# Attention heads in alternating half-array products: the two heads' scores by 64 rows, their products with v by 64 columns in float32

## The chip, the cores and the metric

The kernel runs on one core of a Trainium2 chip. The metric is the device time of one launch in microseconds (us). The time before is 1052.7 us, the median of three runs (1052.44 to 1053.11). The profile is of one more execution, which took 1059.5 us.

## What is computed

Block-causal attention (4 batches, 8 heads, 576 tokens, head dimension 64), and two feed-forward layers on its result (2304 tokens, 512 wide, 2048 in the middle):

```python
scores = 1.0 / np.sqrt(D) * np.matmul(q, k.transpose(0, 1, 3, 2))
mask = (pos[:, None] // 64) >= (pos[None, :] // 64)
scores = np.where(mask, scores, -1000000000.0)
attn = np.exp(scores - np.max(scores, axis=-1, keepdims=True))
attn = attn / (np.sum(attn, axis=-1, keepdims=True) + 1e-09)
x = np.matmul(attn, v)        # then (B, H, S, D) -> (B * S, H * D)
h = x @ moe_w_in;   x = (h * np.cos(h)) @ moe_w_out
h = x @ moe2_w_in;  r = np.maximum(h, 0.0);  out = (r * r) @ moe2_w_out
```

## The kernel before

All matmuls but the transposes and some products with v use float32r operands, each number split into a high part and a low part; a product is then three matmuls, high x high, high x low and low x high, summed in PSUM (`mm3`, L760).

**Order.** The kernel is first recorded as a list of operations with their reads and writes (`Recorder`, L136). A planner (`schedule`, L213) then places them on the engines by assumed costs and priorities, chooses the engine where several can do an operation, and assigns the 8 PSUM banks ("s" for scores, "t" for transposes, "a" for products with v, "h" and "y" for the feed-forward layers; at most five "s" and one "a" at a time). The program on each engine is in the planner's order, and every engine waits in that order. SyncE (SP) alone issues the DMAs.

**Attention.** A unit is a pair of heads of one batch; its 128 rows of transposed q or k hold the first head in rows 0 to 63 (`TOP`) and the second in rows 64 to 127 (`BOT`). Batch 0 is cut into region 1 (tokens 0 to 255, units 0 to 3) and region 2 (tokens 256 to 575, units 4 to 7), so that the feed-forward layer can begin early; batches 1 to 3 are units 8 to 19, each with both regions. `prep` (L856) transposes k and q and splits them: high and low keys `kh`, `kl`, queries `sa`, `sb`. Scores of a block of 128 queries go over 128, 256, 384 or 512 keys; the last 64 tokens of both heads are done together by `tail` tiles. DVE takes the row maximum (`soft_min`), ACT the exponential, POOL mostly the division; the result e is transposed on TensorE (PE) into r1 and r2 (`unit_transpose`, L992), and `unit_av` (L1024) multiplies it with v into xt, which is stored to x_d and split for the first layer.

Two switches decide how a unit is computed. `APART` (L31): in region 1 of batch 0 (and in units below 4) the scores of a head are three 64-row products, one head after the other. In all others, `both` (L864) copies each head's high keys into both halves of a tile (`ka`, `kb`), and its low keys into a tile whose other half is zero (`kz0a` to `kz1b`), by six DMAs per unit, and a head's scores are two products over all 128 rows:

```python
matmul(t[:, o:o + n], u.S[h][:, c], u.K[h][:, 0:n], True, False, holds=(e, st))
matmul(t[:, o:o + n], u.S[h][:, c], u.S[3][h][:, 0:n], False, True)
```

`PLAIN` (L30): units 0 to 7 multiply r with v as plain float32 into 64 columns of PSUM rows, one head after the other, and the profile shows two records for each such product. Units 8 to 19 split r into high and low (`r1l`, `r2l`, on DVE) and v into `vs` (`prep_v`, L841), compute 128 columns (v high and v low) for each, and add the two halves by a copy to `xb` on ACT and an addition on DVE.

k, q and v of a unit have one buffer each (`NATB = 1`, L33). The weights of the first layer arrive as `raw`, in two buffers (L666), and pass through ACT, POOL and DVE.

Of the kernel before, what the change touches and what calls it, by code (L numbers as in the profile page):

```python
# [29 lines left out]
PLAIN = 8  # L30
APART = 4  # L31
E1 = 7
# [313 lines left out]
def kernel(  # L346
# [264 lines left out]
    for i in range(2):  # L611
# [5 lines left out]

        pads = [T(sb, [128, 576], F32R, f"kz{i}{j}") for j in "ab"]
        memset(f(pads[0][64:128]), 0.0)
        memset(f(pads[1][0:64]), 0.0)  # L620
        QS.append((sa, sb_, tails, pads))
# [193 lines left out]
    def load_pair(b, p, part):  # L815
# [3 lines left out]
        u.apart = part == 1 or len(units) < APART  # L819
# [36 lines left out]
    def prep(u):  # L856

        kn, qn, vn = u.nat
        sa, sb_, tails, pads = u.S = QS[u.i % 2]
        ka, kb, kl, kh = u.K = tuple(T(sb, [128, 576], F32R, n, 2) for n in ("ka", "kb", "kl", "kh"))  # L860
# [5 lines left out]
        def both(which):  # L866
            if u.apart:
                return
            for i, h in enumerate((TOP, BOT)):
                if which == "h":  # L870
                    for g in (TOP, BOT):
                        dma(f(u.K[i][g]), f(kh[h]), 147456, 600.0)
                else:
                    dma(f(pads[i][h]), f(kl[h]), 147456, 600.0)

        def queries(t, c):
            if u.apart:

                act(sa[:, c], t, ACTF.Copy, scale=scale)
                stt(sb_[:, c], t, scale, f(sa[:, c]), ALU.mult, ALU.subtract)  # L880
                return
# [13 lines left out]
        else:  # L895
# [7 lines left out]
            both("h")  # L903
            lo_part(kl[:, 512:576], t[:, 0:64], kh[:, 512:576])
            both("l")
# [19 lines left out]
    @of("scores")  # L925
    def unit_scores(u, kind):

        e = T(sb, [128, 576], F32, "e", E1)
        st = T(sb, [128, 8], F32, "st", 6)
        if kind == "P":  # L930
            for j in range(2):
                t = bank("s")
                kc = slice(j * 288, j * 288 + 288)
                (th, tl), kl, kh = u.S[2], u.K[2][:, kc], u.K[3][:, kc]
                for i, (l, r) in enumerate(((th, kh), (th, kl), (tl, kh))):
                    matmul(t[:, 0:288], l, r, i == 0, i == 2, holds=(e, st))
                soft_min(e[:, kc], t[:, 0:288], mask[:, 0:288], st[:, 2 + j:3 + j])
            tt(st[:, 0:1], st[:, 2:3], st[:, 3:4], ALU.min)
            parts = [(0, 576)]
        else:  # L940
            h, ts_ = kind
            half = (TOP, BOT)[h]
            t = bank("s")
            parts, o = [], 0
            for j in ts_:
                n = 128 * (j + 1)
                c = slice(j * 128, j * 128 + 128)
                if u.apart:

                    (qh, ql), (kl, kh) = [x[half, c] for x in u.S[:2]], [x[half, 0:n] for x in u.K[2:]]  # L950
                    for i, (l, r) in enumerate(((qh, kh), (qh, kl), (ql, kh))):
                        matmul(t[:, o:o + n], l, r, i == 0, i == 2, holds=(e, st))
# [425 lines left out]
```

## Time and profile before

| | |
|---|---|
| median of the runs | 1052.7 us |
| profiled execution | 1059.5 us, span 1057.7 us |
| PE busy | 1020.6 us (96%) |
| DVE busy | 698.7 us (66%) |
| ACT busy | 676.7 us (64%) |
| POOL busy | 376.7 us (36%) |

Attention lies in the first 400 us of the span, among the first layer's first half; the rest is feed-forward layers only. A matmul's duration in the profile is from start to modelled end; successive matmuls overlap, so what one costs PE is the distance between starts. The page gives PE a granted clock of 0.9 to 1.0 in each slice.

### The profile page before, as it was taken

To read this page: it belongs to the slowest core of one execution; us is meant where nothing else is said; L and a number is where in the kernel's file an instruction comes from. 1 tells how busy PE (TensorE), PEld (TensorE's weight loads), DVE (VectorE), ACT (ScalarE), POOL (GpSimd) and SP (SyncE) were. 2 spreads that over 40 slices of the span, in tenths; PEclk is the share of its full clock that TensorE was granted. 3 is DMA by queue.
4 is the path that set the end of the run, shared out by engine and by line. 5 is a ranking of instruction groups with operands and counts; after the bars stand their busy time and mean duration, and the time that the engine had idled before them with its cause. 6 is when DMAs were issued, how large, how long until landed. Compare 5 with 4: busy or idle time off the path is not lost.

```text
span 1057.7 us, 18891 instructions
## 1 busy us (share of the span) xinstructions
PE 1020.6 (96%) x6440; PEld 926.8 (88%) x6440; DVE 698.7 (66%) x1805; ACT 676.7 (64%) x1685; POOL 376.7 (36%) x466
## 2 busy tenths in 40 slices
PE   8959999999999999999999999999999999999998
PEld 5657788889899989999889999988989888988987
DVE  4687499886758674567653326999877287747433
ACT  5688689888979886776574336777755364524312
POOL 5336224454545556948982222114120002000000
PEclk9989999999999999999999999999999999999999
DMA  6686534534425124455321223375761383131121
GB/s 156 160 187 165 140 93 120 140 81 119 114 72 126 43 64 136 136 167 189 113 86 63 90 71 119 115 226 156 266 197 53 120 321 98 60 100 51 60 70 40
DMA packets 125919, 129.16 MB, mean 122 GB/s; under 512 B 72832, under 2 KB 99456, under 8 KB 124800
## 3 DMA queue, kind: packets, MB, share of 16 engines
q1 hardware_dynamic: 125824, 127.96, 41.2%
q8 instruction: 51, 0.84, 0.3%
q14 instruction: 44, 0.36, 0.1%
HBM read 81.79 MB, written 31.98 MB: 108 GB/s over the span
## 4 chain that ended last, share of the span: by engine, by line
PE 58%; ACT 12%; DVE 12%; POOL 9%; DMA 5%; issue 4%; SPq 0%; ACTq 0%; DVEq 0%; POOLq 0%
PE y L512 24%; PE h L512 23%; PE a L512 4%; PE t L521 3%; ACT e L397 3%; PE s L512 3%; POOL gl L450 3%; POOL c L691 2%; POOL w L450 2%; DVE e L918 1%; DVE c L413 1%; POOL xl L450 1%; ACT r2h L465 1%; DVE r L406 1%; DVE gl L454 1%
## 5 line engine op out<-in xcount | busy, mean ns | idle before, releaser
L512 PE MATMUL h<-xh,w 128*128 128x256 f32 (+1 forms) x1408 | 288.6, 298 | 0.6 <-ACT u L465 0.4
L512 PEld LDWEIGHTS h<-xh,w 128*128 128x128 f32 x1408 | 231.1, 188 | 4.2 <-ACT u L465 0.9
L512 PE MATMUL y<-gh,w 128*128 128x384 f32 (+2 forms) x896 | 218.3, 318 | 9.1 <-POOL w L431 7.5
L512 PE MATMUL h<-xl,w 128*128 128x256 f32 (+1 forms) x704 | 206.6, 294 | 0.3 <-POOL xl L450 0.3
L512 PE MATMUL y<-w,gh 128*128 128x512 f32 x576 | 182.2, 396 | 0.7 <-ACT gh L436 0.4
L512 PEld LDWEIGHTS y<-gh,w 128*128 128x128 f32 x896 | 156.4, 190 | 12.0 <-POOL w L431 7.7
L512 PE MATMUL y<-gl,w 128*128 128x384 f32 (+2 forms) x448 | 143.0, 321 | 3.3 <-POOL gl L450 3.1
L512 PEld LDWEIGHTS h<-xl,w 128*128 128x128 f32 x704 | 132.4, 188 | 1.4 <-POOL xl L450 0.6
L512 PEld LDWEIGHTS y<-w,gh 128*128 128x128 f32 x576 | 106.9, 187 | 27.1 <-ACT w L436 1.1
L450 POOL TENSOR_TENSOR gl<-r,gh 128x384 fp32r<-128x384 f32 (+2 forms) x95 | 91.1, 963 | 92.9 <-ACT gh L436 92.2
L436 ACT ACTIVATE gh<-r 128x256 fp32r<-128x256 f32 (+2 forms) x192 | 85.6, 446 | 45.4 <-DVE r L1291 30.9
L495 POOL TENSOR_SCALAR e<-e,st 128x128 f32<-128x128 f32 (+4 forms) x144 | 83.8, 592 | 86.2 <-DVE st L975 61.0
L512 PE MATMUL y<-w,gl 128*128 128x512 f32 x288 | 113.4, 395 | 0.2 <-DVE gl L454 0.2
L512 PEld LDWEIGHTS y<-gl,w 128*128 128x128 f32 x448 | 85.0, 190 | 7.3 <-POOL gl L450 6.2
L397 ACT ACTIVATE e<-e,st 128x128 f32<-128x128 f32 (+4 forms) x144 | 83.2, 579 | 10.1 <-DVE st L918 8.3
L406 DVE TENSOR_TENSOR r<-h,r 128x384 f32<-128x384 f32 (+2 forms) x112 | 55.7, 498 | 48.5 <-ACT r L397 48.3
L450 POOL TENSOR_TENSOR xl<-x,xh 128x384 fp32r<-128x384 f32 (+1 forms) x36 | 45.0, 1258 | 117.9 <-ACT xh L436 110.8
L413 DVE SCALAR_TENSOR_TENSOR r<-n,h 128x384 f32<-128x384 int32 (+2 forms) x112 | 55.1, 493 | 38.4 <-ACT n L397 26.5
L397 ACT ACTIVATE n<-h 128x384 int32<-128x384 f32 (+2 forms) x112 | 48.5, 437 | 48.6 <-PE h L512 47.5
L918 DVE CUSTOM_DVE_ANT_0 e<-s,mask 128x288 f32<-128x288 f32 (+4 forms) x160 | 73.1, 476 | 6.7 <-PE s L512 5.0
L521 PE MATMUL t<-ident,e 128*128 128x128 f32 (+1 forms) x400 | 70.7, 288 | 3.1 <-POOL e L495 2.6
L397 ACT ACTIVATE r<-r,halfpi 128x384 f32<-128x384 f32 (+2 forms) x112 | 63.4, 567 | 13.7 <-DVE r L413 13.0
(178 smaller groups left out, 2119.0 us busy)
## 6 DMA issues: line engine op xcount, KB each, us to landing
raw<-in_moe_w_in_dram SPq DMA_DIRECT2D x32, 512.0 KB, 4.3
raw<-in_moe_w_out_dram SPq DMA_DIRECT2D x32, 512.0 KB, 3.8
x<-y_d SPq DMA_DIRECT2D x32, 256.0 KB, 3.0
wi_d<-so SPq DMA_DIRECT2D x32, 256.0 KB, 3.3
w<-wi_d SPq DMA_DIRECT2D x8, 1024.0 KB, 7.5
k<-in_k_dram SPq DMA_DIRECT2D x36, 128.0 KB, 2.6
q<-in_q_dram SPq DMA_DIRECT2D x36, 128.0 KB, 2.7
v<-in_v_dram SPq DMA_DIRECT2D x36, 128.0 KB, 2.8
```

Source lines behind the costliest of these rows:

```text
L397: return nc.scalar.activation(real(out), real(in_), func, **kw)
L406: out.size / 0.96 + 68, lambda: nc.vector.tensor_tensor(real(out), real(a), real(b), op=op), [out], [a, b],
L413: lambda: nc.vector.scalar_tensor_tensor(real(out), real(a), s, real(b), op0=op0, op1=op1),
L436: "ACT": ("ACT", n / 1.2 + 92, lambda: nc.scalar.activation(real(hi), real(x), ACTF.Copy)),
L450: lambda: nc.gpsimd.tensor_tensor(real(lo), real(x), real(f(hi)), op=ALU.subtract), 1,
L454: lambda: nc.vector.tensor_tensor(real(lo), real(x), real(f(hi)), op=ALU.subtract), 1,
L465: "ACT": ("ACT", n / 1.2 + 50, lambda: nc.scalar.activation(real(out), real(ps), ACTF.Copy)),
L495: lambda: nc.gpsimd.tensor_scalar(real(out), real(x), real(s), 1.0, op0=ALU.mult, op1=ALU.mult),
L512: lambda: nc.tensor.matmul(real(ps), lhsT=real(lhsT), rhs=real(rhs), start=start, stop=stop, skip_group_check=True),
L521: lambda: nc.tensor.transpose(real(out), real(in_), real(ident)[0:rows, 0:rows]), [out], [in_, ident],
L691: lambda: nc.gpsimd.tensor_tensor(real(wi), real(t), real(wi), op=ALU.subtract), 1,
L918: lambda: nc.vector.tensor_tensor_reduce(out=real(e), in0=real(ps), in1=real(m), scale=-1.0, scalar=BIG, op0=ALU.add, op1=ALU.min, accum_o ...
```

## The change

For all units: the scores of both heads are three 64-row products per block of queries, alternating between the heads, into two banks; PE gets them as one `block` that the planner doesn't take apart. The products with v are plain float32 for all units, alternating between the heads, into the two halves of one bank, and one copy takes both heads out. The copies `ka`, `kb`, `kz`, the split of r, `vs` and `xb` are no longer used; v is read directly. The two heads' softmax statistics share a tile, so that the small operations on sums come once per block and not once per head.

```diff
-PLAIN = 8
-APART = 4
+PLAIN = 99
...
+    def block(mms, cost, holds=()):
+
+        def fn():
+            for ps, l, r, start, stop in mms:
+                nc.tensor.matmul(real(ps), lhsT=real(l), rhs=real(r), start=start, stop=stop, skip_group_check=True)
+
+        R.op("PE", cost, fn, [m[0] for m in mms], [x for m in mms for x in m[1:3]], holds=holds)
...
-            for s, h in ((sa, TOP), (sb_, BOT)):
-                act(s[h, c], t[h], ACTF.Copy, scale=scale)
-            for s, h, g in ((sa, TOP, BOT), (sb_, BOT, TOP)):
-                stt(s[g, c], t[h], scale, f(s[h, c]), ALU.mult, ALU.subtract)
+
+            act(sa[:, c], t, ACTF.Copy, scale=scale)
+            stt(sb_[:, c], t, scale, f(sa[:, c]), ALU.mult, ALU.subtract)
...
-            both("h")
...
-            both("l")
...
+    @of("scores")
+    def unit_scores(u, rows):
+
+        es = [T(sb, [128, 576], F32, "e", E1) for _ in range(2)]
+        st = T(sb, [128, 12], F32, "st", 6)
+        ts_ = [bank("s") for _ in range(2)]
+        mms, parts, o, cost = [], [[], []], 0, 190
+        for j in rows:
+            n = 128 * (j + 1)
+            c = slice(j * 128, j * 128 + 128)
+            for i in range(3):
+                for h, half in enumerate((TOP, BOT)):
+                    q_, k_ = u.S[i == 2][half, c], u.K[i == 1][half, 0:n]
+                    mms.append((ts_[h][:, o:o + n], q_, k_, i == 0, i == 2))
+                cost += max(110.0, n / 2.2)
...
+        block(mms, cost, (*es, st, *ts_))
...
-        mms = [(c0, c1, kt, r) for c0, c1, kt, rs in mms for r in rs]
-        xb = None if u.plain else T(sb2, [128, 320], F32, "xb", 2)
...
         if u.plain:
-            copy(u.xt[mine, o:o + n], a[mine, 0:n])
-        else:
+
+            a, mms, cost = bank("a"), [], 140
+            for i, (c0, c1, kt, rs) in enumerate(got):
+                rows = slice(0, 64) if kt == 4 else slice(0, 128)
+                cost += max(120.0, 4 * (c1 - c0) / 2.2)
+                for h, half in enumerate((TOP, BOT)):
+                    mms.append((a[half, c0:c1], u.nat[2][rows, kt, h], f(rs[h][0][rows]), i == 0, i == len(got) - 1))
+            block(mms, cost, [u.xt])
+            copy(u.xt[:, o:o + n], a[:, 0:n])
+            return
...
-            for kind, av in UNITS[r]:
-                e = unit_scores(u, kind)
-                unit_transpose(u, kind, e)
-                if av:
-                    unit_av(u, *av)
-                if kind == "P" or (u.part == 1 and av == (0, 1)):
-                    pair(i + 1)
-                    load(i + NATB)
+            if r == 1:
+                u.r1 = [None, None]
+            for rows in [(0, 1)] if r == 1 else [(3,), (2,)]:
+                es = unit_scores(u, rows)
+                for h in range(2):
+                    unit_transpose(u, rows, h, es[h])
+            if r == 2:
+                last_transpose(u, last_scores(u))
+            if r == 2 or u.part == 1:
+                pair(i + 1)
+                load(i + NATB)
+            unit_av(u, r)
```

PE, region 1 of a unit of batch 2, before: products with v of one head (r1h and r1l are the parts of its transposed e, vs the parts of v), then scores of two blocks of queries (sa1, sb1 the queries of the two heads, ka, kb, kz the copied keys; the number behind a name is the tile's).

```order
L512 MATMUL a_1953<-r1h_1893,vs_1578 128x256
L512 MATMUL a_1953<-r1l_1894,vs_1578 128x256
L512 MATMUL a_1953<-r1h_1893,vs_1578 128x128
L512 MATMUL a_1953<-r1l_1894,vs_1578 128x128
L521 MATMUL t_1947<-ident_86,e_1775 128x128
L521 MATMUL t_1961<-ident_86,e_1775 64x128
L512 MATMUL s_1935<-kz1a_110,sa1_153 128x128
L512 MATMUL s_1935<-ka_1765,sa1_153 128x256
L512 MATMUL s_1935<-kz1a_110,sa1_153 128x256
L512 MATMUL s_1942<-kz1b_114,sb1_164 128x128
```

PE, the like of it now (s_1863 and s_1864 are the two heads' banks, r1h_1773 and r1h_1796 their transposed e):

```order
L521 MATMUL a_1826<-r1h_1773,v_1470 64x256
L521 MATMUL a_1826<-r1h_1796,v_1470 64x256
L521 MATMUL a_1826<-r1h_1773,v_1470 64x128
L521 MATMUL a_1826<-r1h_1796,v_1470 64x128
L528 MATMUL t_1839<-ident_86,e_1678 128x128 x4
L528 MATMUL t_1848<-ident_86,e_1679 128x128 x4
L528 MATMUL t_1858<-ident_86,e_1702 128x128 x3
L521 MATMUL s_1863<-kh_1514,sa1_141 128x512
L521 MATMUL s_1864<-kh_1514,sa1_141 128x512
L521 MATMUL s_1863<-kl_1515,sa1_141 128x512
L521 MATMUL s_1864<-kl_1515,sa1_141 128x512
```

Each product now stands next to the other head's; in the products with v both go into one tile a.

SP, weights and batch 0 region 2, before (raw is a piece of the weights as it arrives, k and q a unit's keys and queries, the tail of q landing in k's tile; ka, kb, kz the copies of keys):

```order
L669 DMA raw<-in_moe_w_out_dram 128x4096
L527 DMA k<-in_k_dram 128x4x64
L527 DMA ka<-kh 64x576 x2
L669 DMA raw<-in_moe_w_out_dram 128x4096
L527 DMA kb<-kh 64x576 x2
L527 DMA kz0a<-kl 64x576
L527 DMA kz0b<-kl 64x576
L527 DMA k<-in_k_dram 128x4x64
L527 DMA k<-in_k_dram 64x2x64
L527 DMA q<-in_q_dram 128x4x64 x2
L527 DMA k<-in_q_dram 64x2x64
L669 DMA raw<-in_moe_w_out_dram 128x4096 x4
```

SP, the same pieces of the weights now:

```order
L534 DMA k<-in_k_dram 128x4x64 x2
L534 DMA k<-in_k_dram 64x2x64
L534 DMA k<-in_q_dram 64x2x64
L672 DMA raw<-in_moe_w_out_dram 128x4096 x2
L534 DMA q<-in_q_dram 128x4x64 x2
L672 DMA raw<-in_moe_w_out_dram 128x4096
L534 DMA q<-in_q_dram 128x4x64 x2
L672 DMA raw<-in_moe_w_out_dram 128x4096 x4
```

The copies of keys are gone from between the pieces of the weights.

SP, two units of batch 2 that follow each other, before (x_d is the store of xt, y1_d that of the first layer's result):

```order
L527 DMA x_d_336<-xt_3404 128x256
L527 DMA q_3483<-in_q_dram 128x4x64 x2
L527 DMA k_3387<-in_q_dram 64x2x64
L527 DMA v_3507<-in_v_dram 128x4x64 x2
L527 DMA v_3507<-in_v_dram 64x2x64
L527 DMA y1_d_1359<-y_3520 128x256
L527 DMA v_3507<-in_v_dram 64x2x64
L527 DMA y1_d_1359<-y_3555 128x256
L527 DMA x_d_336<-xt_3404 128x320
```

SP, two such units now:

```order
L534 DMA x_d_301<-xt_3555 128x256
L534 DMA v_3665<-in_v_dram 128x4x64
L534 DMA y1_d_1224<-y_3661 128x320
L534 DMA x_d_301<-xt_3555 128x320
L534 DMA v_3665<-in_v_dram 128x4x64
L534 DMA v_3665<-in_v_dram 64x2x64 x2
```

The next unit's v is loaded around the store of the last unit's region 2, and no longer before it by the loads of q.

## Rows read from the trace of the kernel before

**Rows 1.** The page's first part: each engine's busy time, share, instructions.

```profile
PE 1020.6 (96%) x6440; PEld 926.8 (88%) x6440; DVE 698.7 (66%) x1805; ACT 676.7 (64%) x1685; POOL 376.7 (36%) x466
```

**Rows 2.** Busy time by stretch: length, PE, PEld, DVE, ACT, POOL; clock, DMA share, GB/s.

```profile
0.00:47.00 47.00, 42.04 (x164) 27.36 (x165) 24.77 (x81) 27.69 (x74) 22.75 (x42) 1.00 0.65 165
47.00:145.00 98.00, 85.99 (x532) 70.64 (x531) 73.59 (x200) 77.22 (x176) 36.52 (x45) 0.95 0.59 146
145.00:400.00 255.00, 245.07 (x1795) 230.77 (x1793) 197.58 (x651) 217.87 (x606) 122.28 (x189) 1.00 0.39 99
400.00:1057.70 657.70, 647.46 (x3956) 597.99 (x3954) 402.78 (x875) 353.96 (x830) 195.20 (x192) 1.00 0.38 125
```

**Rows 3.** The chain that ended last, in order of time: start, length, what.

```profile
52.08 5.97 DMA raw<-in_moe_w_in_dram
...
80.73 2.34 PE a L512 x10
...
118.48 2.38 PE a L512 x10
```

**Rows 4.** PE's waits: engine, tile, line and what ended it: total, times, longest.

```profile
PE y L512 <- POOL w L431: 7.5, 1, 7.5
...
PE h L512 <- ACT w L436: 2.9, 1, 2.9
```

**Rows 5.** Timeline of PE, region 1, one head alone: start, length, instruction.

```profile
13.07 0.41 PE L512 MATMUL s<-kl,sa 64*128 64x128 f32 x1
13.28 0.41 PE L512 MATMUL s<-kh,sb 64*128 64x128 f32 x1
...
16.76 1.54 PE L512 MATMUL a<-r1h,v 128*64 128x256 f32 x4
```

**Rows 6.** Timeline of PE, 7.0 to 8.8 us: both heads' 64-row scores.

```profile
8.02 0.41 PE L512 MATMUL s<-kl,sa 64*128 64x256 f32 x1
8.14 0.52 PE L512 MATMUL s<-kh,sa 64*128 64x256 f32 x1
8.23 0.41 PE L512 MATMUL s<-kh,sb 64*128 64x256 f32 x1
8.44 0.30 PE L512 MATMUL s<-kh,sa 64*128 64x128 f32 x1
```

**Rows 7.** Timeline of PE, 37 to 41 us: single 64-row products among others.

```profile
37.56 0.28 PE L512 MATMUL h<-xs1h,w 128*128 128x256 f32 x1
37.77 0.33 PE L512 MATMUL s<-kh,sa 64*128 64x128 f32 x1
38.03 0.55 PE L521 MATMUL t<-ident,e 128*128 128x128 f32 x3
38.51 0.32 PE L512 MATMUL s<-kl,sa 64*128 64x128 f32 x1
...
38.79 0.33 PE L512 MATMUL s<-kh,sa 64*128 64x256 f32 x1
38.96 0.28 PE L512 MATMUL s<-kl,sa 64*128 64x256 f32 x1
```

**Rows 8.** Timeline of PE, 80.5 to 83.2 us: float32 products with v, one head.

```profile
80.66 2.15 PE L512 MATMUL a<-r2h,v 128*64 128x320 f32 x8
82.75 0.32 PE L512 MATMUL a<-r2t,v 64*64 64x64 f32 x2
83.00 0.44 PE L521 MATMUL t<-ident,e 128*128 128x128 f32 x2
```

**Rows 9.** Timeline of PE, 158 us: split products with v, batch 1.

```profile
158.29 0.31 PE L512 MATMUL a<-r2h,vs 128*128 128x320 f32 x1
158.44 0.31 PE L512 MATMUL a<-r2l,vs 128*128 128x320 f32 x1
```

**Rows 10.** Timeline of SP: start, length, DMA issue.

```profile
66.62 1.15 SPq L527 DMA_DIRECT2D ka<-kh  x2
```

**Rows 11.** Groups of DVE from 145 to 400 us: count, busy, mean ns, idle before.

```profile
L406 DVE TENSOR_TENSOR r2l<-t,r2h 128x512 fp32r<-128x512 f32 x36 | 24.8, 688 | 5.7 <-ACT r2h L465 4.8
```

**Rows 12.** DMA issues: count, KB each, median us from issue to landing.

```profile
v<-in_v_dram SPq DMA_DIRECT2D x36, 128.0 KB, 2.8
```

More of the change, by code (lines that the diff above doesn't have):

```diff
@@ L616 @@
             memset(f(t), 0.0)
[L618 to L621, printed above, removed]
+        QS.append((sa, sb_, tails))
     class DView:
@@ L818, in load_pair @@
         u.plain = len(units) < PLAIN
-        u.apart = part == 1 or len(units) < APART
         u.nat = []
@@ L923, in soft_min, with normalized @@
         )
[L925 to L952, printed above, removed]
-                else:
-                    matmul(t[:, o:o + n], u.S[h][:, c], u.K[h][:, 0:n], True, False, holds=(e, st))
-                    matmul(t[:, o:o + n], u.S[h][:, c], u.S[3][h][:, 0:n], False, True)
-                parts.append((o, n))
-                o += n
-            for i, (o, n) in enumerate(parts):
-                soft_min(e[:, o:o + n], t[:, o:o + n], mask[:, 512 - n:512], st[:, i:i + 1])
-        for i, (o, n) in enumerate(parts):
-            x = e[:, o:o + n]
+    def normalized(st, parts):
+        m = len(parts)
+        for i, x in enumerate(parts):
             turn("exp", x, x, ACTF.Exp, bias=st[:, i:i + 1], scale=-1.0, accum_out=st[:, 4 + i:5 + i])
-        m = len(parts)
-        sums = st[:, 4:4 + m]
+        sums, rs = st[:, 4:4 + m], st[:, 8:8 + m]
         flexible(
@@ new lines, in right_parts, with last_transpose @@
+    def right_parts(u):
+        if not hasattr(u, "r2"):
+            names = "h" if u.plain else "hl"
+            u.r2 = [T(sb, [128, 2, 4, 320], F32R, f"r2{i}") for i in names]
+            u.r2t = T(sb, [128, 2, 64], F32R, "r2t")
+    @of("weighted")
+    def last_transpose(u, e):
+        right_parts(u)
+        t = t_tile()
+        for kt in range(4):
+            transpose(t[:, kt * 128:kt * 128 + 128], e[:, kt * 128:kt * 128 + 128], holds=u.r2)
+        src = t.rearrange("p (k h c) -> p h k c", k=4, h=2)
+        parts_of(u, src, [r[:, :, :, 256:320] for r in u.r2])
+        t2 = t_tile()
+        transpose(t2[0:64, 0:128], e[:, 512:576], holds=[u.r2t])
+        parts_of(u, t2[0:64, 0:128].rearrange("p (h c) -> p h c", h=2), [u.r2t[0:64], u.r2t[64:128]])
@@ L1017, in unit_transpose @@
+    @of("weighted")
+    def unit_transpose(u, rows, h, e):
+        t = t_tile()
+        if rows[0] == 0:
+            r1 = [T(sb, [128, 384], F32R, f"r1{i}", 4) for i in ("h" if u.plain else "hl")]
+            u.r1[h] = r1
+            for o in (0, 128, 256):
+                transpose(t[:, o:o + 128], e[:, o:o + 128], holds=r1)
+            parts_of(u, t[:, 0:384], r1)
+            return
+        right_parts(u)
+        n = rows[0] + 1
         for kt in range(n):
             transpose(t[:, kt * 128:kt * 128 + 128], e[:, kt * 128:kt * 128 + 128], holds=u.r2)
-        o = (ts_[0] - 2) * 128
+        o = (rows[0] - 2) * 128
@@ L1023, in unit_av @@
     @of("weighted")
-    def unit_av(u, h, region):
+    def unit_av(u, region):
         if not hasattr(u, "xt"):
@@ L1037, in unit_av @@
[L1037 to L1047 removed]
+                got.append((c, 320, kt, [[r[:, h, kt, c:320] for r in u.r2] for h in range(2)]))
@@ new lines, in unit_av @@
+            block(mms, cost, [u.xt])
+            copy(u.xt[:, o:o + n], a[:, 0:n])
+            return
+        xb = T(sb2, [128, 320], F32, "xb", 2)
+        for h, (mine, other) in enumerate(((TOP, BOT), (BOT, TOP))):
+            a = bank("a")
+            mms = [(c0, c1, kt, r) for c0, c1, kt, rs in got for r in rs[h]]
+            for i, (c0, c1, kt, r) in enumerate(mms):
+                vs = u.vs[:, kt, h].rearrange("p s d -> p (s d)")
+                matmul(a[:, c0:c1], vs, r, i == 0, i == len(mms) - 1, holds=(xb, u.xt))
```

87 lines of the change are left out of this document (30 added, 57 removed).

## The prediction

> **What bounds the kernel now.** I read the page's busy times first, then the same by stretch, the chain, PE's waits, and PE's and SP's timelines. PE is busy 96% of the span [rows 1], but not evenly [rows 2]: it idles 5.0 us of the first 47 (region 1 of batch 0), 12.0 us of the 98 to 145 (region 2, weights of the first layer), 9.9 us of the 255 to 400 (batches 1 to 3), and 10.2 us of the 658 after, which the change does not touch. So time is gained by PE work saved before 400 us, by idle taken away there, or not at all; DVE (197.6 of 255 us) and ACT (217.9) are beside PE, not ahead of it. In the chain of waits a DMA of weights takes 6.0 us from 52 us on, and from 80 us stand the products with v of batch 0, four times 2.34 to 2.38 us, the first and the last of them shown [rows 3].
>
> Prices at PE. A 320-column split product costs 0.15 us, 0.47 ns a column [rows 9]. In float32, one head's four region-2 products (eight records) take 2.09 us and its last one 0.25 [rows 8]. That is the higher of TensorE's two levels (2.4 GHz). Around 13 us it ran at the lower (1.2 GHz): 128-column 64-row products start 0.21 us apart [rows 5], while at 38 us even 256 columns take 0.17 [rows 7]; the granted clock, 1.00 in that stretch [rows 2], does not tell the two apart.
>
> **Do the two heads run at once?** On this all hangs. For rows the trace shows it: where 64-row products of two heads happen to meet, 256-column ones of both start at 8.02, 8.14 and 8.23 us and the next at 8.44 [rows 6]; at the lower level 256 columns alone take 0.21, so three one after the other need 0.64 and stand here within 0.42. For columns no row shows it; before, one bank "a" keeps the heads apart. Bounds: all beside each other (one head's time for both), or none (twice that). I take all, since a float32 record reads a column at half the rate of a split one (269 ns against 147 for 320 columns, from 2.09 less two 192-column records, and [rows 9]), so two such streams ask no more of the reading than one split stream.
>
> The Trainium skill ("TensorE: Matmul & The Clock Gate", Measured speedup vs the span model) gives 2.38x for three column tiles; by that (0.79 of full) a unit's products with v would take 0.8 us more and the time would be 1049, and no run here shows it yet.
>
> **The change part by part.**
>
> *Batches 1 to 3, PE.* Before, a unit's scores are 2 heads x 2 products x 1280 columns (128 + 256 + 384 + 512), 5120 x 0.47 = 2.4 us; its products with v are 2 x (2 x (384 + 1152) + 64) = 6272 columns, 2.9 us. Sum 5.3. After: scores are one stream of 3 x 1280 columns, 1.8 us if weight loads hide, plus 12 x 0.05 if they don't (0.17 us between 256-column products of one head [rows 7] against 0.12 of streaming); I take 2.1. With v: 2.1 + 0.25 [rows 8] for region 2, and 384/1152 of the former, 0.65, for region 1: 3.0 for both heads. Then the change between full and half array: 0.09 us to get in (37.56 to 37.77 against 0.12), some 0.15 in the product and out (37.77 to 38.03, against 0.11) [rows 7]; about 0.2 for each of some four to five blocks, 0.8. Sum 5.9. So +0.5 us x 12 units = +6 us (bounds: -2 with loads hidden and 0.1 a switch, +41 without overlap of columns).
>
> The Trainium skill ("TensorEngine Tiling (Array Packing)", Key Properties) says that a change of tiling mode drains the engine; the trace agrees, with the 0.09 and 0.15 us above, and these are in the sum.
>
> *Batches 1 to 3, other engines.* DVE loses the splits of r (24.8 us for those of 512 columns [rows 11], three per unit, and as many columns again in two of 384 for r2l and two for r1l, so some 50 us), the additions, half of the query splits; POOL and ACT lose vs and xb. They are beside PE, so only PE's idle can come back: 9.9 us at most, nothing at least. I take 8, the whole less a fifth, as this idle lies in a stretch in which DVE and ACT are busy 77% and 85%. -8.
>
> *Batches 1 to 3, a new wait.* v has one buffer and is now read until the unit's last product; before, its split freed it early. In the new order, at 7 of the 11 changes of unit only 20 to 30 rows of PE work (by the prices above about 3 to 5 us, a transpose being at most 0.16, 38.03 to 38.51 for three and a switch [rows 7]) stand between the last use of one v and the first of the next. The load takes 2.8 us to land [rows 12] after two issues of about 0.55, and twice a store of xt stands between them on SP: 4 to 4.6 us. Behind the waiting product stand the transposes and the feed-forward products on PE. 7 x 0.7 = +5 us (bounds 0, where e is late anyway, and 7 x 2.8 = 20).
>
> *Batch 0, region 1 (to 47 us).* 8 heads x 3 x (0.21 + 0.32) of scores, at the lower level (0.32 for 256 columns, being 0.21 and a load) = 12.7, and 8 x 1.3 with v (the 0.65 above, doubled; 1.54 with its last end [rows 5]) = 10.4. At once, up to 11.5 us go; but the feed-forward products that follow need weights, so I take half: -6 (bounds -11.5, 0).
>
> *Batch 0, region 2 (47 to 145 us).* 8 heads x (2.1 + 0.25) with v = 18.8 us; half goes, 9.4, of which the added switches of the score blocks (two per unit, 4 x 2 x 0.2 = 1.6) are taken off: and a little for the 12 us in which PE idles and saves nothing: -7. Bounds -9.4 and +1.6.
>
> *Batch 0, SP.* Six copies per unit go, each 0.57 us of issue [rows 10], 24 of them in batch 0, 14 us of SP, and they stand between pieces of the weights in the order. PE waits 7.5 and 2.9 us for weights here [rows 4]; the pieces also wait for their two buffers, so I take a third: -3 (bounds -10.4, 0).
>
> *After 400 us*: unchanged.
>
> Sum: +6 - 8 + 5 - 6 - 7 - 3 = -13 us, from 1059.5 to 1046.5 in a profiled execution. The median of the runs stands 6.8 us below the profiled one, so 1039.7; I forecast 1040.
>
> **Rivals.**
>
> 1. *The column halves do not run at once.* For it: no row shows them doing so, and each float32 product is two records, the second of which may hold back the other head. Against: the row halves do. Then +3.0 x 12 = 35 us, and batch 0 loses 7 + 3 of its gain, the v wait is hidden (-5): 1040 + 40 = 1080. From half overlap on (1060) the change is slower.
> 2. *The v wait takes the gain.* The coarse blocks need two banks, two e and the products of both heads late; if each of the 7 changes of unit costs PE 2.7 us and not 0.7, that is +14: 1054. Below 2.5 us each the gain remains. For it: v's single buffer; against: in batch 0 v is already held so, and PE there shows no wait for v among its longest [rows 4].
> 3. *TensorE falls to the lower level in the attention stretches.* In the first stretch it was there [rows 5] though PE was busy 42.0 of 47 us [rows 2], with half-array products and transposes. Attention is about 12 x 10 us of the 255 (5.9, 25 transposes and the tails); if a fifth of that ran at half speed, +25: 1065. Against: both halves now work, and feed-forward products stand between.
> 4. *Nothing moves*, since batch 0 is held by the weights' conversion and the rest balances: 1051 to 1054.
>
> **How the numbers follow.** A difference of 0.2% (2.1 us) is what a measurement can tell here. Forecast 66%, with its own range 1022 to 1050. Rival 1, full or half: 13%. Rival 2: 9%. Rival 3: 6%. Rival 4: 6%. The low end: -11.5, -9.4, -10.4 and -10 in batches 1 to 3 would be 41 us, 1011; I take 1017. The high end reaches over rivals 2 to 4 to half of rival 1: 1062. Faster takes the forecast and a little of rival 2, 0.68; within 0.2%: rival 4 and some of 2, 0.08; slower 0.24.
>
> **What would show it.** Right: records of the two heads' products with v starting in pairs, a pair every 0.27 us per 320-column record; 64-row products of two heads within 0.05 us of each other; PE's products with v at about 48 us in sum, from start to start, against about 64; DVE's busy time at least 50 us lower; batches 1 to 3 ending 10 us or more earlier, and the stretch after them as long as before. Wrong: v records 0.27 us apart one by one (rival 1); PE waits "a <- DMA v" of over 2 us each (rival 2); spacing of 0.23 us for 256-column feed-forward products between 145 and 400 us (rival 3); the first y product still at 74 us (rival 4, no gain from SP).

## The result and the profile after

The changed kernel takes 1035.2 us (median of four runs, 1033.3 to 1037.0) against 1052.9 before (1052.4 to 1053.6): 0.983 of it, 95% interval 0.981 to 0.985. The forecast was 1040.

Runs of the kernel before fall in two groups, near 1054 and near 1061 us, and its profile [rows 2] is of the upper one, so its 1059.5 us must not be set against the 1033.3 of the profile after. A profile of the lower group exists of the same program with twelve idle-time transposes added (before_warm, below; 1054.6 us); it is what the one after is compared with where times differ.

The page's first part, after (answers to [rows 1]):

```profile
PE 994.8 (96%) x6576; PEld 888.3 (86%) x6576; DVE 605.9 (59%) x1586; ACT 641.9 (62%) x1602; POOL 348.7 (34%) x436
```

DVE's work is 93 us lower, ACT's 35, POOL's 28. Busy time by stretch after, columns as in [rows 2], with the last cut 26 us earlier, as the span is 26 us shorter:

```profile
0.00:47.00 47.00, 33.90 (x190) 24.34 (x190) 27.07 (x83) 33.18 (x86) 22.47 (x40) 0.82 0.66 173
47.00:145.00 98.00, 86.65 (x628) 71.44 (x628) 70.05 (x219) 79.25 (x197) 37.85 (x50) 0.97 0.39 103
145.00:374.00 229.00, 228.80 (x1821) 196.52 (x1820) 105.31 (x406) 176.39 (x496) 96.93 (x159) 1.00 0.25 66
374.00:1031.50 657.50, 645.46 (x3941) 595.99 (x3939) 403.42 (x879) 353.11 (x826) 191.50 (x189) 1.00 0.39 124
```

From 145 to 374 us PE is never idle (228.8 of 229.0); DVE fell there from 77% of the stretch to 46%. In the first 47 us PE is idle more than before (13.1 us against 5.0). That the last stretch is as long as it was (657.5 against 657.7) follows from the choice of the cut; the marks below compare it.

PE's longest waits after, up to 47 us and from 47 to 145 us (answers to [rows 4]):

```profile
PE t L528 <- POOL e L494: 6.6, 5, 3.1
PE t L528 <- DMA k<-in_k_dram: 3.2, 1, 3.2
PE h L511 <- ACT w L435: 2.1, 1, 2.1
```

```profile
PE y L511 <- POOL w L430: 3.8, 3, 2.1
PE y L511 <- ACT w L435: 3.2, 3, 2.2
PE h L511 <- ACT w L435: 1.6, 1, 1.6
```

and from 145 to 374 us the whole list:

```profile
PE a L521 <- ACT r2h L464: 0.2, 1, 0.2
```

In the first stretch the longest waits are for the normalised e, in the second for weights, in more and shorter pieces than before; the wait for v that I had put down at 5 us does not occur. In the chain the products with v of one head [rows 3] have become those of a pair of heads:

```profile
113.03 2.35 PE a L521 x20
```

Twenty records in the 2.35 us in which ten ran before.

To see where the time came from, both programs are cut at the same marks: the last product with v of region 1, of batch 0, and of all (the first of a view by stretch is before_warm, then after).

```profile
0.00:39.90 39.90, 37.13 (x178) 25.33 (x178) 24.03 (x81) 27.59 (x74) 22.42 (x42) 1.00 0.75 189
39.90:118.50 78.60, 66.45 (x395) 51.34 (x392) 59.21 (x166) 64.07 (x149) 34.49 (x41) 0.93 0.69 168
118.50:391.70 273.20, 263.72 (x1926) 249.20 (x1924) 211.66 (x683) 231.13 (x631) 125.08 (x191) 1.00 0.38 96
391.70:1052.80 661.10, 649.27 (x3961) 598.66 (x3960) 403.36 (x875) 354.74 (x831) 191.65 (x192) 1.00 0.38 124
```

```profile
0.00:39.90 39.90, 29.05 (x154) 19.96 (x154) 22.03 (x72) 26.41 (x71) 20.18 (x37) 0.79 0.66 172
39.90:115.30 75.40, 62.31 (x456) 50.40 (x452) 51.18 (x147) 60.95 (x142) 33.47 (x39) 0.95 0.48 128
115.30:369.20 253.90, 253.19 (x2003) 217.21 (x1999) 129.22 (x488) 200.10 (x560) 102.73 (x170) 1.00 0.25 65
369.20:1031.50 662.30, 650.26 (x3975) 600.73 (x3973) 403.42 (x879) 354.46 (x829) 192.37 (x190) 1.00 0.39 124
```

The steps take 0.0, 3.2, 19.3 and -1.2 us less, 21.3 in sum; 17.7 remains between the medians (after's profile is 1.9 below its median, before_warm's 1.7 above that of before).

The planner also moved feed-forward products across these marks, and that must be taken out first. Counted in PE's order, batches 1 to 3 hold 264,704 columns of h and y products after, 277,760 before: 13,056 x 0.47 ns = 6.1 us of work went elsewhere, net 4.3 into batch 0 (12,288 columns more in region 2, 3,072 fewer in region 1) and 1.8 behind the last mark. So batches 1 to 3 gained 13.2 us: PE busy 10.5 less, 6.1 of it moved, so 4.4 of work; and idle 9.5 to 0.7, so 8.8. Region 2 of batch 0 gained 3.2 + 5.8 = 9.0. Region 1 gained nothing (it lost 1.4): PE's busy time there went from 37.1 us, 2.7 of them the twelve added transposes, to 29.1, and its idle from 2.8 to 10.9.

### The profile page after: what moved, and what is told of

Its sections match the earlier page's. It is cut to its first block, busy times and chain, and to the rows that moved or that the text cites. A ratio compares the mean times of both kernels' runs of the same rounds, so it can differ in the third digit from the quotient of the medians.

```text
span 1031.5 us, 18593 instructions
## 1 busy us (share of the span) xinstructions
PE 994.8 (96%) x6576; PEld 888.3 (86%) x6576; DVE 605.9 (59%) x1586; ACT 641.9 (62%) x1602; POOL 348.7 (34%) x436
## 4 chain that ended last, share of the span: by engine, by line
PE 73%; POOL 8%; DVE 8%; ACT 5%; DMA 3%; issue 2%; SPq 0%; DVEq 0%; POOLq 0%; ACTq 0%
PE y L511 31%; PE h L511 27%; PE t L528 6%; PE a L521 5%; PE s L521 3%; POOL gl L449 3%; POOL c L694 2%; DMA raw<-in_moe_w_in_dram 2%; POOL w L449 2%; DVE c L412 1%; DVE gl L453 1%; PE s L511 1%; DVE r L405 1%; DVE r L1289 1%; ACT r L396 1%
## 5 line engine op out<-in xcount | busy, mean ns | idle before, releaser
L511 PE MATMUL y<-gh,w 128*128 128x384 f32 (+2 forms) x896 | 219.0, 321 | 11.5 <-POOL w L430 3.8
L449 POOL TENSOR_TENSOR gl<-r,gh 128x384 fp32r<-128x384 f32 (+2 forms) x93 | 88.8, 961 | 123.2 <-ACT gh L435 122.5
L412 DVE SCALAR_TENSOR_TENSOR r<-n,h 128x384 f32<-128x384 int32 (+2 forms) x112 | 55.1, 493 | 70.4 <-ACT n L396 59.0
L901 DVE CUSTOM_DVE_ANT_0 e<-s,mask 128x384 f32<-128x384 f32 (+4 forms) x160 | 70.9, 480 | 33.6 <-PE s L521 24.6
L405 DVE TENSOR_TENSOR r<-h,r 128x384 f32<-128x384 f32 (+2 forms) x112 | 55.6, 498 | 50.1 <-ACT r L396 49.9
L449 POOL TENSOR_TENSOR xl<-x,xh 128x384 fp32r<-128x384 f32 (+1 forms) x32 | 39.1, 1228 | 122.7 <-ACT xh L435 115.6
L528 PE MATMUL t<-ident,e 128*128 128x128 f32 (+1 forms) x400 | 65.0, 287 | 7.5 <-POOL e L494 6.9
```

The lines of the kernel that those rows point to most:

```text
L405: out.size / 0.96 + 68, lambda: nc.vector.tensor_tensor(real(out), real(a), real(b), op=op), [out], [a, b],
L412: lambda: nc.vector.scalar_tensor_tensor(real(out), real(a), s, real(b), op0=op0, op1=op1),
L449: lambda: nc.gpsimd.tensor_tensor(real(lo), real(x), real(f(hi)), op=ALU.subtract), 1,
L511: lambda: nc.tensor.matmul(real(ps), lhsT=real(lhsT), rhs=real(rhs), start=start, stop=stop, skip_group_check=True),
L901: lambda: nc.vector.tensor_tensor_reduce(out=real(e), in0=real(ps), in1=real(m), scale=-1.0, scalar=BIG, op0=ALU.add, op1=ALU.min, accum_o ...
```

## The experiments

The ratios are to the kernel before, timed beside each version. Because of its two groups its median there lies between 1055.1 and 1060.5, and the ratios carry that spread; versions of the changed kernel are compared with 1035.2, differences under 2 us not read. The lower group of before lies at 1054.1 to 1054.5 beside the versions and at 1052.9 beside the changed kernel, so a version can look up to 1.6 us slower than it is. Behind the last product with v the profiles differ by themselves: the same 1,399,744 columns of feed-forward products take from 662.1 us (after) to 667.0 (fill_wt).

### Do the column halves run at once: v_apart

```diff
-            block(mms, cost, [u.xt])
+            block(mms[0::2] + mms[1::2], cost, [u.xt])
```

> The changed kernel with, in each block of products with v, all records of head 0 before all of head 1; everything else stands as it was, all other engines' orders too. Theory (the two column halves run at once only because their instructions stand next to each other, and PE is the bound of batches 1 to 3): a unit's 3.0 us with v become 6.0, 12 x 3.0 = 36 us in batches 1 to 3 and half of 4 x 3.0 in batch 0, so 1035 + 42 = 1077 us, and 320-column records 0.27 us apart one by one. Rival (the gain is relief of DVE, ACT and POOL, not PE's work; PE has slack in those stretches): 1035 to 1040 us. Second rival (PE runs the halves side by side whatever their order in the block): 1035 us.

Measured: 1071.2 us, 1.011 of before (1.006 to 1.016). The same instructions in another order cost 36 us. PE's timeline after, region 2 of a unit in batch 1:

```profile
156.97 2.16 PE L521 MATMUL a<-r2h,v 128*64 128x320 f32 x16
```

and with the heads apart:

```profile
162.32 0.88 PE L521 MATMUL a<-r1h,v 128*64 128x256 f32 x8
...
168.11 2.15 PE L521 MATMUL a<-r2h,v 128*64 128x320 f32 x8
170.19 0.32 PE L521 MATMUL a<-r2t,v 64*64 64x64 f32 x2
170.45 2.15 PE L521 MATMUL a<-r2h,v 128*64 128x320 f32 x8
```

Sixteen records take 2.16 us in pairs and twice 2.15 apart: the halves overlap fully. Without that the change would be slower than before. The 6 us by which the time stays under the 1077 expected are region 1: there four records of one head stand ahead of four of the other, and all eight still take 0.88 us, in pairs.

The Trainium skill ("TensorE: Matmul & The Clock Gate", Measured speedup vs the span model) gives 2.38x for three column tiles; for two the trace shows 4.3 / 2.16, the full 2.0.

### Does it matter where the 64-row products stand: scores_apart

```diff
-        block(mms, cost, (*es, st, *ts_))
+        block(mms[0::2] + mms[1::2], cost, (*es, st, *ts_))
```

> The changed kernel with, in each block of 64-row scores, all products of head 0 before all of head 1; everything else stands. Theory (row halves run at once only next to each other, and each head's weight loads hide only behind the other head's product): a unit's scores go from 2.2 us to 2 x (1.8 + 12 x 0.05) = 4.8, so 12 x 2.6 = 31 us in batches 1 to 3 and half of 4 x 2.6 in batch 0: 1071 us. Rival (relief of the other engines is the gain): 1035 to 1040. If only the streaming and not the loads counts, 2 x 1.8 = 3.6 a unit, 1054.

Measured: 1038.0 us, 0.979 (0.973 to 0.985): 3 us more than after, not 36. Both numbers expected for the theory failed; the number is in the range of the rival, but the timeline shows another reason. PE's timeline of a region-1 block, in whose program order all six products of head 0 stand before those of head 1:

```profile
168.44 0.32 PE L521 MATMUL s<-kh,sa 64*128 64x128 f32 x1
168.60 0.27 PE L521 MATMUL s<-kl,sa 64*128 64x128 f32 x1
168.71 0.27 PE L521 MATMUL s<-kh,sb 64*128 64x128 f32 x1
168.72 0.44 PE L521 MATMUL s<-kh,sa 64*128 64x128 f32 x2
168.89 0.39 PE L521 MATMUL s<-kl,sa 64*128 64x128 f32 x2
169.00 0.27 PE L521 MATMUL s<-kh,sb 64*128 64x128 f32 x1
169.11 0.33 PE L521 MATMUL s<-kh,sa 64*128 64x256 f32 x1
169.11 0.28 PE L521 MATMUL s<-kh,sb 64*128 64x256 f32 x1
169.28 0.28 PE L521 MATMUL s<-kl,sa 64*128 64x256 f32 x1
169.40 0.28 PE L521 MATMUL s<-kh,sb 64*128 64x256 f32 x1
```

Head 1's first product starts at 168.72, before three 256-column ones of head 0 that stand ahead of it (the rows with x2 hold one record of each head; head 0's last starts at 169.11). In blocks of three products a head the pairs are complete. So PE itself brings the row halves together when the other head's products stand a few places behind; ten records of one head ahead of the other's, as with v in region 2, are too many.

The Trainium skill ("TensorE: Matmul & The Clock Gate", The mechanism) says that matmuls start and end strictly in program order. These start records differ from that; ends are modelled in the trace and say nothing.

### What the relief of the vector engines is worth: dead_vector and split_v

```diff
             copy(f(rs[0]), src)
+            if u.i >= 8:
+                lo_part(rs[1], src, rs[0])
...
+                for mine, other in ((TOP, BOT), (BOT, TOP)):
+                    copy(xb[mine, 0:n], a[other, 0:n])
+                    tt(xb[mine, 0:n], a[mine, 0:n], xb[mine, 0:n], ALU.add)
```

> The changed kernel with dead work on the vector engines in batches 1 to 3: the low parts of the transposed e, which nothing reads, and the copies and additions of the two halves of the products with v, into a tile that nothing reads (about as much DVE and ACT work as the change took away there, some 75 us; v's own split on POOL is not put back). PE's instructions are the same. Theory (PE's 9.9 us of waits in batches 1 to 3 came from the load on DVE and ACT and are given back by its relief): they come back, 1035 + 8 = 1043 us, with PE waits on r2h, e and sa again. Rival (the waits came from the order of before, in pieces of one head at a time; the other engines have room): 1035 to 1037 us.

Measured: 1046.8 us, 0.988 (0.983 to 0.993).

```diff
-PLAIN = 99
+PLAIN = 8
```

> The changed kernel with the old split products with v in batches 1 to 3 (high and low parts of the transposed e and of v, full array, two halves added afterwards); scores and batch 0 stay as changed. Against the run with dead vector work (1046.8 us) it differs in PE's products with v and in v's split on POOL and ACT. Theory (PE saves 0.27 us a unit by float32 column halves, and most of what v's new form brings is the work it takes off DVE and ACT): 1046.8 + 3 = 1048 to 1051 us. Rival (the prediction's price: float32 halves cost PE 0.1 us more than split products, and two changes of array each unit on top): 1040 to 1045 us.

Measured: 1041.4 us, 0.986 (0.981 to 0.991), in the rival's range. Batches 1 to 3 in the two (first dead_vector, then split_v; their stretches begin and end with the same products as 115.3:369.2 above):

```profile
112.80:380.20 267.40, 261.92 (x2026) 220.36 (x2024) 196.62 (x625) 215.67 (x597) 109.79 (x185) 1.00 0.24 62
```

```profile
114.60:378.80 264.20, 260.17 (x2003) 239.85 (x2003) 198.79 (x621) 218.73 (x599) 123.50 (x190) 1.00 0.24 63
```

In both DVE is back near 197 us and PE's idle time back at 5.5 and 4.0, from 0.7. That vector work keeps PE waiting is shown, and dead_vector's rival (the other engines have room) refuted; how much it is worth is not exact. With dead work the whole is 11.6 us longer; with the real split products, which load DVE, ACT and POOL as much or more, only 6.2. Of the 13.4 us by which dead_vector's batches 1 to 3 are longer, 4.8 are idle time; 4.9 are feed-forward products (7,104 columns that stand behind the last mark in after), and 3.1 are the 399 transposes, the same in both, in another order (45.1 us from start to start, after 42.0). The dead steps hold the single bank "a" longer, which is a likely reason for the order and was not tested.

In split_v the products with v take 41.3 us from start to start in batches 1 to 3 without waits, after 38.3: the float32 halves save 0.25 us a unit, so the rival's price for them is wrong though its number came out. But the transposes take 40.0 us there and 42.0 after: 2 of the 3 us come back beside the half-array blocks, as the rival had it with its changes of array. Of the gain in batches 1 to 3, the new form of v's products is 6 us; the remaining 7 are put down to scores and copies by subtraction alone, and the shared softmax statistics were not tested by themselves.

### Which batches gain: new_batch0 and new_batches13

Both run the old and the new functions side by side, chosen by unit:

```diff
+NEW = range(8)
...
+        u.new = len(units) in NEW
```

In the second `NEW` is `range(8, 99)`.

> The change in batch 0 alone (its eight steps); batches 1 to 3 run as before, with split products with v, copied keys and one head at a time. Theory (the two parts add up, and batch 0 gives what its marks in the traces show, 9.7 us until the last product with v of batch 0, the rest is batches 1 to 3): 9 to 10 us below before. Rival 1 (batch 0 is held by the weights' conversion; what PE gets done earlier there is waited away): 0 to 3 us below. Rival 2 (the gain is in batch 0 as the prediction's terms of -6, -7 and -3 have it): 16 us below.

Measured: 1052.6 us, 0.995 (0.992 to 0.998): 1.5 us below the lower group of before, 9 below the upper. Its ten runs, 1049.9 to 1054.9, show no groups.

> The change in batches 1 to 3 alone; batch 0 runs as before. Theory (relief of DVE and ACT, some 10 us, and about 9 us less PE work in scores and products with v, some of it lost to the changes between full and half array and to feed-forward work that comes due elsewhere): 10 to 14 us below before, and with the run of batch 0 alone the sum is the whole gain of 18 to 21. Rival (the prediction's terms, +6 -8 +5): 0 to 3 us above.

Measured: 1044.3 us, 0.990 (0.983 to 0.996), its four runs in two groups (1040.5 and 1041.6; 1047.0 and 1048.7), as batch 0 is that of before. Each group is 13 us below the like one of before. With the 1.5 us of batch 0 against the lower group that makes 14.5, 3 short of the whole.

The traces show where the 3 us are. Batches 1 to 3, first with the change in batch 0 alone, then with the change in them alone (cut at the last products with v, as above):

```profile
115.70:387.70 272.00, 260.52 (x1891) 244.87 (x1892) 209.15 (x679) 227.81 (x628) 126.61 (x197) 1.00 0.39 97
```

```profile
117.60:376.00 258.40, 257.88 (x2039) 221.97 (x2038) 130.46 (x484) 202.44 (x566) 101.81 (x169) 1.00 0.25 64
```

In new_batch0 the end of batch 0 comes 2.7 us earlier than in before_warm, with 10,176 more columns of h and y done (4.8 us): a lead of 7.5, as in the whole change (3.2 and 4.3). But batches 1 to 3, with that much less to do, take only 1.2 us less (272.0 against 273.2): PE idles 11.5 us in them instead of 9.5, and the attention's products there take 1.5 more. Rival 1's number came out, but the lead was lost behind batch 0 and not in it. In new_batches13 batches 1 to 3 take 14.8 us less with 2,112 columns fewer (1.0 us), a gain of 13.8 like the 13.2 of the whole change, and PE is idle for 0.5. Where PE is never idle, work done earlier counts in full; by this reading batch 0's gain needs the change in batches 1 to 3.

### Why before has two groups: before_again and before_warm

> The kernel before, profiled a second time: its first profiled execution was 1059.5 us, 6.8 above the median of its runs, while the profiled execution of the changed kernel is one of its fast ones. If the 6.8 us lay in one place of the first 400 us (a late DMA of weights in batch 0, as the 7.5 us wait of PE for a weight suggests), the last product with v now ends near 392 to 394 us instead of 399.4 and the wait is gone or shorter. If they lay nowhere in particular, every mark is earlier by the same 0.6%: 397 us for the last product with v, 660 for the last y of the first layer.

Measured: one run, 1063.1 us, last product with v at 400.0: the marks repeat within 1 us, and the wait of 7.5 us for a weight is there too. Neither reading held.

```diff
+    fills = {0: 9, 17: 3}
...
+            for _ in range(n):
+                nc.tensor.transpose(real(out), real(ident), real(ident))
```

The numbers are 9 transposes ahead of the first and 3 ahead of a later one.

> The kernel before with 9 transposes of a constant at its start, where PE has nothing to do until 3.2 us, and 3 more ahead of the first transposes of the second unit's keys (a wait of 0.5 us). Runs of the kernel before fall in two groups, near 1054 and near 1061 us, and both its profiles (1059.5 and 1063.1) show TensorE at the lower level until 33 us, while a kernel with the same batch 0 and a lower time shows the higher one from 16 us. Theory (the groups are when TensorE comes to its higher level in the first 47 us): with PE busy from the start all runs come near 1054 or below, and the profile shows transposes of 0.27 us from 16 us on or earlier, region 1 done at 39 us instead of 47. Rival (the groups have another cause, a DMA of weights): two groups as before, region 1 at 47 us in the profile of a slow one.

Measured: 1058.8 us, 1.001 (0.998 to 1.004), twelve runs still in two groups. As a cure it failed. But its profile fell in the lower group, and the same two transposes of e (a row of the timeline) and the same 17 us (a row by stretch) show the cause (first before_warm, then before):

```profile
22.05 0.44 PE L528 MATMUL t<-ident,e 128*128 128x128 f32 x2
20.00:37.00 17.00, 16.70 (x95) 11.45 (x96) 14.25 (x43) 15.84 (x43) 9.50 (x16) 1.00 0.80 206
```

```profile
23.73 0.69 PE L521 MATMUL t<-ident,e 128*128 128x128 f32 x2
20.00:37.00 17.00, 17.00 (x55) 10.51 (x54) 10.01 (x30) 9.23 (x27) 7.37 (x12) 1.00 0.45 122
```

PE is busy in both, with 95 products in one and 55 in the other. In the lower group TensorE is at the higher level (2.4 GHz) from 19.2 us, in the upper one at the lower (1.2 GHz) until 37: 256-column products start 0.21 us apart at 34 us and 0.12 from 37.2 on. Region 1's last product with v starts at 39.8 instead of 47.2, and the lead of 7.4 us is still 7.6 at the last product with v of all. The other two profiles with this batch 0 agree: before_again, in the upper group, rises at 38 us, and new_batches13, in its lower one, at 18. Before_warm and before had PE busy without a gap over 0.1 us from 9.7 to 36 us; what decides was not found. The granted clock is printed as 1.00 for these 17 us in both, so that here only the spacing shows the level; in after, 0.50 is printed for 33 to 37 us, where the spacing is 0.21 too.

### What holds batch 0: norm_dve, fill, dead_copies, fill_wt

```diff
-FREE = {"hi": "POOL ACT", "lo": "DVE POOL", "copy": "ACT DVE", "norm": "POOL", "abs": "DVE", "wt": "POOL DVE", "eps": "ACT DVE", "add": "DVE POOL"}
+FREE = {"hi": "POOL ACT", "lo": "DVE POOL", "copy": "ACT DVE", "norm": "POOL DVE", "abs": "DVE", "wt": "POOL DVE", "eps": "ACT DVE", "add": "DVE POOL"}
```

> The changed kernel with one constant changed: the normalisation of e, until now on POOL alone, may go to DVE where the planner expects it to end earlier there. PE waits 6.9 us for POOL's e in batch 0, 3.1 of them in one, and DVE now has room. Theory (that wait is the longest left before 145 us and goes with it, and POOL converts the weights sooner): 3 to 6 us less, 1029 to 1032 us. Rival (what PE waits for next are the weights, whose conversion by ACT and POOL is unchanged, and in batches 1 to 3 PE is never idle): 1034 to 1037 us.

Measured: 1036.0 us, 0.981 (0.976 to 0.985). Region 1's last product with v starts at 36.7 us instead of 39.8, and nothing came of it, as the rival had it. The planner made another order here: by the end of batch 0 12,224 fewer columns of h and y are done than in after, 5.7 us of work, and it ends 5.7 us earlier, so the lead of 3 us was lost in region 2.

The fill uses before_warm's lines with 9, 26, 8 and 16 transposes.

> The changed kernel with transposes of a constant, whose results are overwritten, put where PE idles in batch 0: 9 at the start (until 3.2 us PE has nothing to do), 26 ahead of the first transpose of e (a wait of 3.15 us), 8 and 16 ahead of two later ones (0.9 and 1.9 us). In the changed kernel TensorE comes to its higher level at 11.4 us, falls back in the wait and stays at the lower until 24 us. Theory A (region 1 of batch 0 is held by TensorE's level): at the higher one its 9.2 us from 15 to 24 us shrink to about 5, and the kernel gains 3 to 5 us: 1031. Theory B (what is gained in the first 47 us is waited away at the weights, whose conversion holds batch 0; that is why the normalisation on DVE, with region 1 done 3.1 us earlier, changed nothing): region 1 ends earlier and the time stays within 2 us, 1034 to 1037.

Measured: 1034.4 us, 0.978 (0.974 to 0.982). After, PE waited here and fell back to the lower level:

```profile
11.22 0.67 PE L528 MATMUL t<-ident,q 128*128 128x128 f32 x3
15.03 1.36 PE L528 MATMUL t<-ident,e 128*128 128x128 f32 x4 [3.15 <-POOL e L494]
```

Filled, it is at the higher one for the rest of region 1:

```profile
12.09 4.36 PE L534 MATMUL t<-ident 128*128 128x128 f32 x26
16.29 1.16 PE L535 MATMUL t<-ident,e 128*128 128x128 f32 x6
```

Region 1's last product with v starts at 37.3, and the median is that of after within 1 us: theory B's number. Batches 1 to 3 and the rest of the filled profile, cut as above:

```profile
112.00:366.40 254.40, 253.75 (x2003) 217.08 (x2001) 129.41 (x488) 200.17 (x560) 102.86 (x170) 1.00 0.25 65
366.40:1031.60 665.20, 652.14 (x3975) 600.83 (x3973) 405.80 (x879) 354.79 (x829) 189.45 (x190) 1.00 0.38 123
```

Theory B's reason does not hold. The order is that of after, and the lead of 2.5 us is 3.2 at the end of batch 0 and still 2.8 at the last product with v: nothing of it is waited away at the weights. It is lost behind that, between 605 and 850 us, where the two programs have the same products, within what that part differs by itself. In before, too, the 7.4 us of the level came through. Whether the filling is worth nothing or up to 3 us stays open.

```diff
+            for d, h in zip(ds, (TOP, BOT)):
+                for g in (TOP, BOT):
+                    dma(f(d[g]), f(kh[h]), 147456, 600.0)
...
+            for d, h in zip(ds[2:], (TOP, BOT)):
+                dma(f(d[h]), f(kl[h]), 147456, 600.0)
```

> The changed kernel with the six DMA copies of keys per unit put back into tiles that nothing reads (in all units with full keys, 16 of 20). Theory (the copies' issues on SP stand before pieces of the weights and of q, and the prediction took 3 us for that in batch 0; in batches 1 to 3 nothing waits for SP): 1035 + 1 to 4 us, first y product later than 57 us. Rival 1 (SP has room, the weights wait for their buffers and their conversion): 1034 to 1037 us. Rival 2 (the copies alone explain the wait of 7.5 us for a weight before the first y): 8 us or more.

Measured: 1040.3 us, 0.985 (0.980 to 0.989), 5 us more, just above the theory's 1 to 4. The first y product comes at 62.6 us, where it was 57.1, and in batches 1 to 3 the longest wait of PE is now

```profile
PE a L521 <- DMA v<-in_v_dram: 2.3, 4, 1.2
```

So SP's copies did cost time, and the wait for v, absent in after, is there as soon as SP has more to issue. But the time is not lost where the theory put it: batch 0 ends 0.8 us earlier than in after with 2,880 columns less done (1.4 us), which is a loss of 0.6, while batches 1 to 3 take 6.7 us more with these columns to do, a loss of 5.3, 2.8 of them idle.

```diff
-        R.any([alts[e] for e in FREE[kind].split()[:1 if kind == "wt" and R.phase < 2 else 9]], w, r)
+        R.any([alts[e] for e in FREE[kind].split()], w, r)
```

> The kernel with the filled waits and one rule changed: the subtraction in the conversion of the first layer's weights, until now on POOL alone, may go to DVE where the planner expects it to end earlier there. PE waits 3.7 + 3.3 + 2.6 us for weights of POOL and ACT before 145 us, and with the waits filled region 1 ended 2.5 us earlier without gain. Theory (batch 0 is held by the weights' conversion on POOL): these waits shrink and what region 1 gained comes through, 3 to 6 us below the filled kernel: 1028 to 1031. Rival (conversion is held by ACT, by the two buffers of raw pieces and their DMAs, not by POOL): 1033 to 1036, the waits for w as long as before, now with ACT or DVE at their end.

Measured: 1047.7 us, 0.991 (0.988 to 0.994), 13 us worse than filled, against both readings. PE's timeline at the first y products:

```profile
67.28 0.41 PE L511 MATMUL y<-gl,w 128*128 128x256 f32 x1
67.50 0.41 PE L511 MATMUL y<-gh,w 128*128 128x256 f32 x1
```

PE now waits for ACT's part of the pieces (7.3 us in six waits before 145 us), and 256 columns take 0.21 us, the lower level, between the waits (67.28 to 67.50). DVE did all 16 subtractions, in 0.75 us each instead of POOL's 1.29, and the first y came no earlier than in fill (55.1 in both): that POOL's subtraction is what holds batch 0 is refuted. What does stays open. PE's longest waits there are for weights, and norm_dve lost its lead in region 2; but fill kept its lead.

No version beat the changed kernel by more than the measurement can tell.

## Why the prediction was right or wrong

The number was right (4.8 us off) and so was the claim that carries it, that both halves run at once. The sum behind it was wrong in several terms that offset each other, so that it came so close is in good part luck.

- **Column halves**: right. A pair of 320-column records every 0.27 us, as said; v_apart prices the rival at +36 us, where I had 35 and 7 + 3 more.
- **+6 for PE's work in batches 1 to 3**: the step that failed most; it is -4.4. The unit after was well priced (5.9; from start to start 29.9 us of scores and 38.3 with v in twelve units, 5.7, and 0.25 more in the transposes and tails beside them, which went from 50.1 to 53.1 us). The unit before was not: I took every product at 0.47 ns a column, 5.3 us, and it measures 34.9 + 41.3 us in twelve without waits, 6.35. Single products stood among others there, and the first of each costs more, as in before at 157 us:

```profile
156.96 0.41 PE L512 MATMUL a<-r2h,vs 128*128 128x320 f32 x1 [0.43 <-ACT r2h L465]
157.21 0.46 PE L512 MATMUL y<-gh,w 128*128 128x320 f32 x2
...
159.57 0.42 PE L512 MATMUL s<-ka,sa 128*128 128x384 f32 x1
159.83 0.34 PE L512 MATMUL s<-kz1a,sa 128*128 128x384 f32 x1
160.00 0.30 PE L512 MATMUL s<-kh,tail1h 128*128 128x288 f32 x1
```

  A 320-column split product that follows another kind holds PE 0.20 us (0.25 behind a wait, as here), not 0.15 [rows 9]; the first of two 384-column scores 0.26, the second 0.17. Of the 12 us by which the twelve units stand above streaming, 8 lie in such first products.
- **-8 for PE's idle time**: right, 8.8 of 9.5 came back; dead_vector and split_v bring 3 to 5 us of idle time back with the vector work.
- **+5 for v's single buffer**: 0. Only dead_copies shows the wait at any size (2.3 us; other versions 0.8 at most). The 7 close changes of unit are there, with 3.3 to 4.5 us between the last product with one v and the first with the next. But in after SP, without the copies, issues the load within 0.1 us of that last product, and it lands 2.4 us later (median); I had put two issues and a store ahead of it.
- **-6 for region 1**: 0. PE's work shrank by 5.4 us (37.1 less the 2.7 of added transposes, to 29.1), and all of it became waiting, for the normalised e (POOL), for k and for weights. I halved the gain for weights; the whole was due. It was also priced from a profile at the lower level, the state in which those 6.8 us above the median were lost: the two were the same microseconds, counted once as a saving and once as an offset.
- **-7 for region 2 and -3 for SP**: 9.0 together (3.2 between the marks and 5.8 of work moved there). SP's part was put in the wrong place: dead_copies costs 0.6 us in batch 0 and 5.3 in batches 1 to 3.
- **After 400 us**: right.

Expected -13, of which +3 in batches 1 to 3 and -16 in batch 0; found 13.2 in batches 1 to 3 and 7.5 in batch 0, which alone are worth only 1.5 (new_batch0). Rival 3 (the lower level in the attention stretches) did not happen from 145 to 374 us, where PE is never idle and the granted clock is 1.00; in region 1 TensorE was at the lower level until 11.4, from 15 to 25 and from 33 to 39 us, and what that cost is open (fill). Of the signs, the products with v went from 70.0 to 53.5 us from start to start (64 to 48 forecast), DVE lost 93 us (50), and y's first start moved from 74 (66.7 in the lower group) to 57.1 us.

## What to carry to other kernels

Two products that each use half of the array run in the time of one if they stand next to each other; check that in the order, for columns above all, as ten records in between cost everything that the halves gain. Price what is removed from records where they stand, not from streaming rates: the unit of before, strewn in pieces among other products, cost PE a fifth more than its columns stream. And before a gain is priced in one stretch, ask which wait follows it: of the 5 us that PE saved in region 1 nothing was left at its end, and batch 0's lead of 7.5 us was worth 1.5 as long as batches 1 to 3 were those of before.

## What the runs showed of the hardware

- 64-row products of the other half start ahead of older ones of the first half: at 168.72 us before three that stand ahead of them in the program.
- Column halves overlap fully in float32 in one PSUM bank: 16 records in 2.16 us. With four records of one head ahead of the other's four they still do (eight in 0.88 us), with ten they do not (twice 2.15).
- The same order of work, but for twelve added transposes, has TensorE at the higher level from 19 us in one run and from 37 us in another, 7.4 us apart at the end of region 1, with PE busy from 9.7 to 36 us in both. The granted clock is printed as 1.00 from 20 to 37 us in both and does not show it.
